# Attention and routed experts on one core: the first batch's expert is guessed from summed values, and work is moved in the written order

## The chip, the core and the metric

The kernel runs on one core of one Trainium2 chip. The metric is the device time of one execution in microseconds (us). TensorE (PE) multiplies matrices, VectorE (DVE), ScalarE (ACT) and GpSimd (POOL) work on tiles, and SyncE (SP) issues most transfers. TensorE's clock has two levels, 1.2 and 2.4 GHz; the profile gives the granted clock as a share of the higher one.

## What is computed

```python
k_p = k.reshape(B, H, Sp, pool, D).mean(axis=3)      # 8 batches, 8 heads, 576 rows, 64 wide, pool 8
v_p = v.reshape(B, H, Sp, pool, D).mean(axis=3)
attn = softmax(scale * q @ k_p.T) @ v_p
x = attn.transpose(0, 2, 1, 3).reshape(B * S, H * D)  # 4608 tokens of 512
g_idx = argmax(x @ w_group); g_w = softmax(...)[g_idx]            # one of 4 groups
e_idx = argmax(x @ w_expert[g_idx]); e_w = softmax(...)[e_idx]    # one of 4 experts in it
out = g_w * e_w * (relu(x @ w1[g, e]) @ w2[g, e])                 # 512 -> 1024 -> 512
```

## The kernel before

The eight batches are worked off one after another. For each batch the attention is computed in five chunks of rows (four of 128 and one of 64), its tokens are routed, and all 576 tokens are run through one expert, the batch's main expert. Tokens of other experts are collected and done in a loop at the end (class Left). The weights and the tokens are each split into a rounded high part and a low part, and three products (high by high, low by high, high by low) replace one exact product.

While batch b runs through its expert, the attention of batch b+1 is computed in the gaps. This order is written out by hand: the strings START, FIRST (batch 0), SECOND (batch 1), STEADY and LAST list pieces of work, `run` (L859) calls them in that order, and each engine gets its instructions in the order in which the pieces issue them (ScalarE from batch 1 on is ordered by the scheduler). In a piece's name the letter says whose it is: `a` attention of the current batch, `m` its expert, `n` the next batch, `w` the next batch's expert, `x` the batch after that, `t` shared. Engines run their queues in order, so a piece that waits holds back all that is behind it on the same engine.

The pieces that matter here:

- `load_k`, `load_v`, `load_q`, `load_qb` (L175 to L219) load keys, values and queries; SP issues them, and ACT a few at the start.
- `kr` (L221) sums eight keys to one by three additions, of two of five column groups (`kr:0`) or three (`kr:1`), on VectorE unless told otherwise; `kt` (L260) turns the sums. `vr` (L240) and `vm` (L245) do the same for values on GpSimd. For batch 0 `vsum` (L250) sums the values on TensorE instead, by eight products with the identity.
- `qt` or `qb` turn queries; `sc`, `mx`, `sb`, `su_`, `nm`, `pt` are the scores, their largest, the exponentials, the sums, the division and the turning of one chunk; `av` and `avd` (L341, L359) multiply by the values and write the tokens' high and low parts.
- `rt`, `route` (L363, L372) give each token its expert by some twenty short VectorE instructions; `count` (L407) counts tokens by expert on TensorE.
- The main expert must be known before its weights can be loaded. For batches 0 and 1 it is guessed from the mean of the values: `guess_x` (L431) multiplies the summed values by small matrices, `guess_r` (L439, batch 0) does so with the unsummed values, `guess_e` (L451) takes the best expert, and SP reads it into a register (L427). Later batches use `main_expert` (L414) after routing.
- `m.load`, `m.cast`, `m.lo`, `m.split` (L503 to L526) load a quarter of a weight matrix, make its high part on ScalarE and its low part on GpSimd. `up` (L528) makes 128 of the 1024 hidden columns for half the tokens with twelve matmuls into one of three PSUM buffers, `upd` (L543) writes the low part of the result on VectorE and so frees the buffer, `down` (L554) is the second layer.
- `warm` (L849) runs matmuls of ones into a PSUM tile that nothing reads.

Of the kernel before, what the change touches and what calls it, by code (L numbers as in the profile page):

```python
# [8 lines left out]
F32 = mybir.dt.float32  # L9
# [25 lines left out]
t.load_wr a.load_k:p a.load_q:0 a.load_v:2 a.load_q:1 a.load_q:4  # L35
t.warm:7 t.turn_wr t.warm:1 a.kr:0 a.qt:0 a.kr:1 a.kt a.sc:0 a.qt:1 a.mx:0 a.sb:0 a.sc:1:m a.mx:1 a.guess_r a.sb:1 a.su_:0 a.nm:0:p a.qt:2 a.guess_e
m.load:1:0 m.load:1:1 m.load:1:2 m.load:1:3 a.vsum n.load_v n.load_k a.su_:1 a.nm:1:p a.pt:0 a.pt:1 a.sc:2:m m.cast:1:0 m.lo:1:0:p:2 a.mx:2 a.sb:2 a.av:0:256
m.cast:1:1 m.lo:1:1:p:2 a.avd:0:256 t.split_wr
# [16 lines left out]
n.pt:3 m.down:4 n.su_:4 n.nm:4:p m.down:5 m.store:1 n.pt:4 x.kr:0 n.av:256:320 n.avd:256:320 x.kr:1 m.down:6 n.rt:256:320 m.down:7 n.route m.down:8 m.store:2 m.down:9 n.main_expert w.load:1:0 w.load:1:1 w.load:1:2 w.load:1:3 m.down:10
x.qb:0 n.gates n.keep_x x.vr:0 x.kt m.down:11 m.store:3 w.split:1:0:p:2 w.load:2:0 x.sc:0 x.mx:0 x.sb:0 x.qb:1 m.down:12 w.split:1:1:p:2 w.load:2:1 x.su_:0 x.nm:0:p m.down:13 m.store:4 x.vr:1 x.vm
# [25 lines left out]
def attn_moe(ctx: ExitStack, tc: tile.TileContext, q, k, v, wg, we, w1, w2, out):  # L82
# [81 lines left out]
    def bc(x, z):  # L164
        return x.unsqueeze(len(x.shape)).broadcast_to(list(x.shape) + [z])

    class Att:
# [203 lines left out]

        def route(s):  # L372

            b = s.b
# [8 lines left out]
            def top1(l, pre):  # L383
                x = sm.tile([128, NC], F32, name="m")
                red(out=x, in_=l, axis=AX.X, op=ALU.max)
                d = sm.tile([128, NC, 4], F32, name="d" + pre)
                tt(out=d, in0=l, in1=bc(x, 4), op=ALU.subtract)
                r = sm.tile([128, NC, 4], F32, name="r" + pre)
                stt(out=r, in0=d, scalar=0.0, in1=desc4.unsqueeze(1).broadcast_to([128, NC, 4]), op0=ALU.is_ge, op1=ALU.mult)
                x = sm.tile([128, NC], F32, name="m2")  # L390
                red(out=x, in_=r, axis=AX.X, op=ALU.max)
                oh = sm.tile([128, NC, 4], F32, name="o" + pre)
                tt(out=oh, in0=r, in1=bc(x, 4), op=ALU.is_equal)
                return oh, d
# [101 lines left out]
    class Moe:  # L496
# [31 lines left out]
        def up(s, f, hf):  # L528
# [303 lines left out]
    class Top:  # L832
# [72 lines left out]
```

## Time and profile before

| | us |
|---|---|
| median of three runs | 587.7 |
| lowest and highest of them | 579.74, 588.12 |
| the profiled execution | 582.81 |
| its span, first to last instruction | 581.1 |

Busy shares of the span: PE 92%, DVE 61%, POOL 42%, ACT 36%. In a table by stage a row has the stretch in us from the span's start, its length, then for PE, PEld (weight loads of TensorE), DVE, ACT and POOL the busy time with the number of instructions, the granted clock, the mean busy share of the transfer engines and GB/s. In a timeline row stand the start, the duration (of all instructions merged into the row), the engine, the line, the operation, the tile written and those read, the shape, the count and, in brackets, how long the engine had been idle and what ended that. L12 is line 12 of the kernel.

### The profile page before, as it was taken

To read this page: it belongs to the slowest core of one execution; us is meant where nothing else is said; L and a number is where in the kernel's file an instruction comes from. 1 tells how busy PE (TensorE), PEld (TensorE's weight loads), DVE (VectorE), ACT (ScalarE), POOL (GpSimd) and SP (SyncE) were. 2 spreads that over 40 slices of the span, in tenths; PEclk is the share of its full clock that TensorE was granted. 3 is DMA by queue.
4 is the path that set the end of the run, shared out by engine and by line. 5 is a ranking of instruction groups with operands and counts; after the bars stand their busy time and mean duration, and the time that the engine had idled before them with its cause. 6 is when DMAs were issued, how large, how long until landed. Compare 5 with 4: busy or idle time off the path is not lost.

```text
span 581.1 us, 15029 instructions
## 1 busy us (share of the span) xinstructions
PE 535.4 (92%) x6081; PEld 462.4 (80%) x6081; DVE 353.7 (61%) x1029; ACT 210.5 (36%) x405; POOL 245.0 (42%) x208
## 2 busy tenths in 40 slices
PE   8988869985999999899989998999999998999995
PEld 3867757765987789789978897889878997899864
DVE  4366567876777587646854595729565672458602
ACT  1234413342322364335532544145423543244111
POOL 2048513256233198136640766075704772231300
PEclk9689979995999999999999999999999999999999
DMA  9179507681706549464843668095746310562831
GB/s 234 33 211 255 89 27 207 178 188 41 179 5 118 175 128 243 75 170 150 229 73 128 186 195 130 30 382 172 162 77 220 101 36 1 181 192 102 276 113 50
DMA packets 114720, 83.44 MB, mean 144 GB/s; under 512 B 69674, under 2 KB 90154, under 8 KB 114264
## 3 DMA queue, kind: packets, MB, share of 16 engines
q1 hardware_dynamic: 110144, 74.37, 48.1%
q10 hardware_dynamic: 4472, 8.04, 4.0%
q8 instruction: 49, 0.80, 0.6%
q14 instruction: 23, 0.19, 0.1%
q0 software_dynamic: 32, 0.04, 0.0%
HBM read 77.14 MB, written 28.38 MB: 182 GB/s over the span
## 4 chain that ended last, share of the span: by engine, by line
PE 75%; DVE 13%; DMA 3%; ACT 3%; issue 2%; POOL 2%; SPq 1%; DVEq 0%; ACTq 0%; POOLq 0%
PE mm L539 29%; PE mm L565 23%; PE sc L300 4%; PE sc L352 4%; PE mm L576 4%; PE tp L369 2%; DMA q<-in_q_dram 2%; POOL w L522 1%; PE tp L444 1%; PE tp L254 1%; DMA sw<-in_moe_w_dram 1%; PE tp L279 1%; DVE xt L361 1%; POOL p L331 1%; PE tp L352 1%
## 5 line engine op out<-in xcount | busy, mean ns | idle before, releaser
L539 PE MATMUL mm<-xt,w 128*128 128x256 f32 (+1 forms) x1536 | 210.6, 295 | 10.0 <-DVE y L582 3.2
L522 POOL TENSOR_TENSOR w<-sw,w 128x1024 fp32r<-128x1024 f32 (+1 forms) x79 | 148.7, 1899 | 163.6 <-ACT w L516 163.6
L539 PEld LDWEIGHTS mm<-xt,w 128*128 128x128 f32 x1536 | 198.7, 194 | 18.2 <-DVE y L582 3.6
L565 PE MATMUL mm<-w,ht 128*128 128x512 f32 x768 | 177.3, 383 | 0.0
L565 PEld LDWEIGHTS mm<-w,ht 128*128 128x128 f32 x768 | 141.5, 189 | 21.6 <-issue 1.9
L541 ACT ACTIVATE ht<-mm 128x256 fp32r<-128x256 f32 (+1 forms) x128 | 52.0, 409 | 96.7 <-PE mm L539 96.5
L331 POOL TENSOR_TENSOR p<-p,su 128x576 f32<-128x576 f32 (+1 forms) x37 | 39.7, 1072 | 104.4 <-DVE su L326 100.8
L516 ACT CAST w<-sw 128x1024 fp32r<-128x1024 f32 x64 | 66.1, 1043 | 23.6 <-DMA sw<-in_moe_w_dram 18.2
L551 DVE SCALAR_TENSOR_TENSOR ht<-mm,ht 128x160 fp32r<-128x160 f32 (+2 forms) x192 | 38.8, 257 | 34.5 <-ACT ht L541 34.0
L311 DVE TENSOR_REDUCE mx<-sc 128x8 f32<-128x576 f32 (+1 forms) x38 | 26.1, 688 | 38.7 <-PE sc L300 38.7
L318 ACT ACTIVATE p<-p 128x576 f32<-128x576 f32 (+1 forms) x40 | 25.5, 637 | 53.4 <-DVE p L316 51.3
L570 ACT ACTIVATE y<-mm,gm 128x512 f32<-128x512 f32 x32 | 21.9, 685 | 58.8 <-PE mm L565 57.4
L352 PE MATMUL sc<-pT,v 32*64 32x256 f32 (+1 forms) x384 | 26.9, 409 | 10.1 <-DVE xt L361 8.1
L547 DVE SCALAR_TENSOR_TENSOR ht<-mm,ht 128x256 fp32r<-128x256 f32 x64 | 26.0, 407 | 15.6 <-ACT ht L541 15.2
L300 PE MATMUL sc<-kT,qT 64*32 64x72 f32 x2176 | 30.6, 229 | 4.0 <-DVE qT L286 2.9
L300 PEld LDWEIGHTS sc<-kT,qT 64*32 64x32 f32 x2176 | 23.9, 105 | 11.7 <-issue 7.4
L338 DVE STREAM_TRANSPOSE pT<-p 128x640 f32<-128x640 f32 (+1 forms) x40 | 30.4, 760 | 3.9 <-POOL p L331 3.9
L324 DVE TENSOR_REDUCE su<-p 128x8 f32<-128x576 f32 (+1 forms) x40 | 27.1, 677 | 5.9 <-ACT p L318 5.7
L576 PE MATMUL mm<-w,ht 128*128 128x512 f32 x128 | 29.6, 381 | 0.0
L352 PE MATMUL tp<-pT,v 32*64 32x256 f32 (+1 forms) x384 | 28.4, 409 | 0.0
L316 DVE TENSOR_TENSOR p<-sc,mx 128x576 f32<-128x576 f32 (+1 forms) x38 | 26.4, 694 | 1.4
L576 PEld LDWEIGHTS mm<-w,ht 128*128 128x128 f32 x128 | 23.9, 189 | 3.8 <-issue 0.5
(203 smaller groups left out, 490.4 us busy)
## 6 DMA issues: line engine op xcount, KB each, us to landing
sw<-in_moe_w_dram SPq DMA_DIRECT2D x72, 512.0 KB
xscr<-xt SPq DMA_DIRECT2D x8, 2304.0 KB
vv<-in_v_dram SPq DMA_DIRECT2D x29, 320.0 KB
q<-in_q_dram SPq DMA_DIRECT2D x112, 72.0 KB
kv<-in_k_dram SPq DMA_DIRECT2D x14, 512.0 KB
out_dram<-y ACTq DMA_DIRECT2D x24, 256.0 KB
pT<-xscr SPq DMA_DIRECT2D x4, 1152.0 KB
out_dram<-y SPq DMA_DIRECT2D x8, 256.0 KB
```

Source lines behind the costliest of these rows:

```text
L300: nc.tensor.matmul(ps[x][32 * g:32 * g + 32, SP * t:SP * t + SP], lhsT=s.qT[c][64 * x:64 * x + 64, g, 32 * t:32 * t + 32], rhs=s.kT[64 * x ...
L324: red(out=su, in_=p.rearrange("p t (x s) -> p t x s", x=2), axis=AX.X, op=ALU.add)
L331: (nc.vector if eng == "v" else nc.gpsimd).tensor_tensor(out=p, in0=p, in1=bc(s.su[c][:, 0:w], SP), op=ALU.mult)
L338: nc.vector.transpose(out=s.pT[:, :, o:o + n].rearrange("p j (t i) -> p t j i", i=32), in_=probs[(s.b * NC + c) % 2][:, 0:n // 32].rearran ...
L352: nc.tensor.matmul(banks[a][64 * x:64 * x + 64, 0:n], lhsT=s.v6[32 * a:32 * a + 32, 5 if x and i == 0 else j, :], rhs=s.pT[32 * a:32 * a + ...
L516: nc.scalar.copy(out=s.w[m, j][0], in_=raw)
L522: (nc.vector if eng == "v" else nc.gpsimd).tensor_tensor(out=wl[:, i:i + n], in0=s.raw[m, j][:, i:i + n], in1=wh[:, i:i + n].bitcast(F32), ...
L539: nc.tensor.matmul(ps[:, 0:n], lhsT=l[:, kc, fs], rhs=apart(xt[:, r, kc, sl]), start=(kc == 0 and i == 0), stop=(kc == 3 and i == 2))
L541: nc.scalar.activation(out=halves(ht[:, sl]), in_=joined(ps[:, 0:n]), func=AF.Relu)
L551: stt(out=ht[:, at:at + hi - lo], in0=ps[:, a, lo:hi], scalar=0.0, in1=ht[:, t + lo:t + hi].bitcast(F32), op0=ALU.max, op1=ALU.subtract)
L565: nc.tensor.matmul(ps, lhsT=s.ht[f][:, 640 * l + o:640 * l + o + 128], rhs=apart(s.w[2, f // 2][r][:, f % 2, :]), start=(i == 0), stop=(i ...
L576: nc.tensor.matmul(ps, lhsT=s.ht[f][:, 512:640], rhs=apart(s.w[2, f // 2][r][:, f % 2, :]), start=(i == 0), stop=(i == 15))
```

## The change

- START: batch 0's values are loaded ahead of its queries and summed on VectorE by a new form of `vr` (all five column groups, three additions), `vm` follows on GpSimd, and the guess uses `guess_x` on the sums. `guess_r` and `vsum` are removed. The guess comes ahead of the second chunk's scores' softmax. `warm` matmuls are half as wide (256 columns), and there are more of them.
- FIRST: batch 1's key sums (`n.kr`) move ahead, from behind the routing to beside `avd` and `upd`; `route` is cut into `route_g` (group) and `route_e` (expert), with expert work between; `count`, `guess_x` and `guess_e` move back by some pieces. Batch 2's key and value sums (`x.kr`, `x.vr`, `x.vm`) move from behind `avd` and from SECOND to ahead of `n.av:256:320`. The division of two chunks moves from GpSimd to VectorE (`:p` to `:v`).
- SECOND: `route_e` and `count` of batch 1 come between its first `up` pieces; `x.vr`, `x.vm` move ahead, `x.kr:1` moves behind `n.route`; two divisions move to VectorE.
- `up` goes through the whole depth for high by high, then high by low part of the tokens, and the weights' low part last.

```diff
@@ -32,28 +32,28 @@
 START = """
-t.load_wr a.load_k:p a.load_q:0 a.load_v:2 a.load_q:1 a.load_q:4
-t.warm:7 t.turn_wr t.warm:1 a.kr:0 a.qt:0 a.kr:1 a.kt a.sc:0 a.qt:1 a.mx:0 a.sb:0 a.sc:1:m a.mx:1 a.guess_r a.sb:1 a.su_:0 a.nm:0:p a.qt:2 a.guess_e
-m.load:1:0 m.load:1:1 m.load:1:2 m.load:1:3 a.vsum n.load_v n.load_k a.su_:1 a.nm:1:p a.pt:0 a.pt:1 a.sc:2:m m.cast:1:0 m.lo:1:0:p:2 a.mx:2 a.sb:2 a.av:0:256
-m.cast:1:1 m.lo:1:1:p:2 a.avd:0:256 t.split_wr
+t.load_wr a.load_k:p a.load_v:2 a.load_q:0 a.load_q:1 a.load_q:4
+t.warm:16 t.turn_wr t.warm:3 a.kr:0 a.kr:1 a.vr:2:f a.kt t.warm:4 a.qt:0 a.qt:1 t.warm:1 a.guess_x a.vm a.sc:0 a.mx:0 a.sb:0 a.guess_e a.sc:1:m
+m.load:1:0 m.load:1:1 m.load:1:2 m.load:1:3 a.mx:1 a.sb:1 a.su_:0 a.nm:0:p a.qt:2 t.warm:4 n.load_v n.load_k a.su_:1 a.nm:1:p a.pt:0 t.warm:6 a.pt:1 m.cast:1:0 m.lo:1:0:p:2 a.sc:2:m
+a.av:0:256 a.mx:2 a.sb:2 m.cast:1:1 m.lo:1:1:p:2 a.avd:0:256 t.split_wr
 FIRST = """
-m.up:5:0 a.pt:4 n.vr:0 m.cast:2:0 m.lo:2:0:p:2 m.upd:5:0 m.up:6:0 m.upd:6:0 m.up:7:0 a.av:256:320 m.upd:7:0 a.rt:0:256 a.avd:256:320
-n.vr:1 n.vm m.up:0:1 m.upd:0:1 a.rt:256:320 m.cast:2:1 m.lo:2:1:p:2 m.up:1:1 m.upd:1:1 m.up:2:1 a.route m.upd:2:1 m.up:3:1 m.cast:2:2 m.lo:2:2:p:2 m.upd:3:1 n.kr:0 n.kr:1 m.up:4:1 a.count m.upd:4:1
-n.guess_x n.kt m.up:5:1 m.upd:5:1 n.guess_e m.cast:2:3 m.lo:2:3:p:2 w.load:1:0 w.load:1:1 n.qb:0 m.up:6:1 m.upd:6:1 n.sc:0 n.mx:0 n.sb:0 n.qb:1 a.gates a.keep_x m.up:7:1 m.upd:7:1
-m.down:0 n.su_:0 n.nm:0:p w.load:1:2 m.down:1 w.load:1:3 m.down:2 n.sc:1 n.mx:1 n.sb:1 n.pt:0 n.qb:2 m.store:0 x.load_v x.load_k m.down:3 w.split:1:0:p:2 n.su_:1 n.nm:1:p m.down:4 n.sc:2 n.mx:2 n.sb:2 n.pt:1 n.qb:3
-m.down:5 m.store:1 w.split:1:1:p:2 n.su_:2 n.nm:2:p n.av:0:256 n.avd:0:256 m.down:6 n.sc:3 n.mx:3 n.sb:3 n.pt:2 n.qb:4 m.down:7 n.su_:3 n.nm:3:v n.rt:0:256 m.down:8 m.store:2
-n.sc:4 n.mx:4 n.sb:4 n.pt:3 w.load:2:0 w.load:2:1 x.load_qb:0 m.down:9 n.su_:4 n.nm:4:v m.down:10 n.pt:4 m.down:11 m.store:3 x.load_qb:1 x.load_qb:2 x.load_qb:3 n.av:256:320 n.avd:256:320 x.kr:0 m.down:12 n.rt:256:320 x.kr:1 m.down:13 m.store:4 n.route
+m.up:5:0 a.pt:4 n.vr:0 m.cast:2:0 m.lo:2:0:p:2 m.upd:5:0 m.up:6:0 m.upd:6:0 m.up:7:0 a.av:256:320 m.upd:7:0 n.kr:0 a.rt:0:256 a.avd:256:320
+n.vr:1 n.vm m.up:0:1 m.upd:0:1 n.kr:1 a.rt:256:320 m.cast:2:1 m.lo:2:1:p:2 m.up:1:1 m.upd:1:1 m.up:2:1 a.route_g m.upd:2:1 m.up:3:1 m.cast:2:2 m.lo:2:2:p:2 a.route_e m.upd:3:1 m.up:4:1 m.upd:4:1
+n.kt m.up:5:1 m.upd:5:1 a.count n.guess_x m.cast:2:3 m.lo:2:3:p:2 n.qb:0 m.up:6:1 n.guess_e w.load:1:0 w.load:1:1 m.upd:6:1 n.sc:0 n.mx:0 n.sb:0 n.qb:1 a.gates a.keep_x m.up:7:1 m.upd:7:1
+m.down:0 n.su_:0 n.nm:0:p w.load:1:2 m.down:1 w.load:1:3 n.sc:1 n.mx:1 n.sb:1 n.pt:0 n.qb:2 m.down:2 m.store:0 x.load_v x.load_k m.down:3 w.split:1:0:p:2 n.su_:1 n.nm:1:v m.down:4 n.sc:2 n.mx:2 n.sb:2 n.pt:1 n.qb:3
+m.down:5 m.store:1 w.split:1:1:p:2 n.su_:2 n.nm:2:v n.av:0:256 n.avd:0:256 m.down:6 n.sc:3 n.mx:3 n.sb:3 n.pt:2 n.qb:4 m.down:7 n.su_:3 n.nm:3:v n.rt:0:256 m.down:8 m.store:2 x.vr:0
+n.sc:4 n.mx:4 n.sb:4 n.pt:3 w.load:2:0 w.load:2:1 x.load_qb:0 m.down:9 n.su_:4 n.nm:4:v m.down:10 n.pt:4 x.kr:0 x.kr:1 x.vr:1 x.vm m.down:11 m.store:3 x.load_qb:1 x.load_qb:2 x.load_qb:3 n.av:256:320 n.avd:256:320 m.down:12 n.rt:256:320 m.down:13 m.store:4 n.route_g
 SECOND = """
-m.up:0:0 m.upd:0:0 m.split:1:2:p:2 m.load:2:2 m.up:1:0 m.upd:1:0 m.split:1:3:p:2 m.load:2:3 m.up:0:1 a.count m.upd:0:1 n.vr:0 m.split:2:0:p:2 m.up:1:1 m.upd:1:1 a.gates a.keep_x m.up:2:0 m.upd:2:0 n.vr:1 n.vm m.up:2:1
+m.up:0:0 m.upd:0:0 m.split:1:2:p:2 m.load:2:2 a.route_e m.up:1:0 m.upd:1:0 m.split:1:3:p:2 m.load:2:3 m.up:0:1 m.upd:0:1 m.split:2:0:p:2 m.up:1:1 a.count m.upd:1:1 a.gates a.keep_x m.up:2:0 m.upd:2:0 m.up:2:1
-n.su_:2 n.nm:2:p m.split:2:3:p:2 m.up:7:1 m.upd:7:1 m.down:0 n.av:0:256 n.avd:0:256 m.down:1 n.sc:3 n.mx:3 n.sb:3 n.pt:2 n.qb:4 m.down:2 m.store:0 n.su_:3 n.nm:3:p x.load_qb:0 x.load_qb:1 x.load_qb:2 x.load_qb:3 m.down:3 n.rt:0:256 n.sc:4 n.mx:4 n.sb:4
-n.pt:3 m.down:4 n.su_:4 n.nm:4:p m.down:5 m.store:1 n.pt:4 x.kr:0 n.av:256:320 n.avd:256:320 x.kr:1 m.down:6 n.rt:256:320 m.down:7 n.route m.down:8 m.store:2 m.down:9 n.main_expert w.load:1:0 w.load:1:1 w.load:1:2 w.load:1:3 m.down:10
-x.qb:0 n.gates n.keep_x x.vr:0 x.kt m.down:11 m.store:3 w.split:1:0:p:2 w.load:2:0 x.sc:0 x.mx:0 x.sb:0 x.qb:1 m.down:12 w.split:1:1:p:2 w.load:2:1 x.su_:0 x.nm:0:p m.down:13 m.store:4 x.vr:1 x.vm
+n.su_:2 n.nm:2:p m.split:2:3:p:2 m.up:7:1 m.upd:7:1 m.down:0 n.av:0:256 n.avd:0:256 m.down:1 n.sc:3 n.mx:3 n.sb:3 n.pt:2 n.qb:4 m.down:2 m.store:0 n.su_:3 n.nm:3:v x.load_qb:0 x.load_qb:1 x.load_qb:2 x.load_qb:3 m.down:3 n.rt:0:256 n.sc:4 n.mx:4 n.sb:4
+n.pt:3 m.down:4 n.su_:4 n.nm:4:v m.down:5 m.store:1 n.pt:4 x.kr:0 n.av:256:320 n.avd:256:320 x.vr:0 m.down:6 n.rt:256:320 m.down:7 n.route x.kr:1 m.down:8 m.store:2 x.vr:1 x.vm m.down:9 n.main_expert w.load:1:0 w.load:1:1 w.load:1:2 w.load:1:3 m.down:10
+x.qb:0 n.gates n.keep_x x.kt m.down:11 m.store:3 w.split:1:0:p:2 w.load:2:0 x.sc:0 x.mx:0 x.sb:0 x.qb:1 m.down:12 w.split:1:1:p:2 w.load:2:1 x.su_:0 x.nm:0:p m.down:13 m.store:4
@@ -237,25 +237,16 @@
                 s.v6 = wk.tile([128, 6, D], F32, name="v6", bufs=2)
             return s.v6
-        def vr(s, u):
-            z = slice(0, 2) if u == 0 else slice(2, 5)
-            a = s.fold(s.v[:, z], nc.gpsimd)
-            nc.gpsimd.tensor_tensor(out=s.vtile()[:, z], in0=a[:, :, 0:64], in1=a[:, :, 64:128], op=ALU.add)
+        def vr(s, u, eng="p"):
+            e = nc.vector if eng == "f" else nc.gpsimd
+            z = (slice(0, 2), slice(2, 5), slice(0, 5))[u]
+            a = s.fold(s.v[:, z], e)
+            e.tensor_tensor(out=s.vtile()[:, z], in0=a[:, :, 0:64], in1=a[:, :, 64:128], op=ALU.add)
         def vm(s):
             for z, at in ((1, 5), (0, 2)):
                 nc.gpsimd.tensor_tensor(out=s.v6[:, at, :], in0=s.v6[:, 2, :], in1=share[:, z:z + 1].broadcast_to([128, D]), op=ALU.mult)
-
-        def vsum(s):
-
-            ps = ps_t.tile([128, 512], F32, name="tp")
-            for j in range(8):
-                nc.tensor.matmul(ps[:, 0:NC * D], lhsT=ident, rhs=s.v[:, :, D * j:D * j + D], start=(j == 0), stop=(j == 7))
-            v6 = s.vtile()
-            nc.scalar.copy(out=v6[:, 0:NC], in_=ps[:, 0:NC * D].rearrange("p (j d) -> p j d", d=D))
-            for z, at in ((1, 5), (0, 2)):
-                nc.scalar.activation(out=v6[:, at, :], in_=ps[:, 2 * D:3 * D], func=AF.Copy, scale=share[:, z:z + 1])
         def kt(s):
             ps = [ps_t.tile([128, 512], F32, name="tp") for i in range(2)]
@@ -369,8 +360,24 @@
+        def top1(s, l, pre):
...
         def route(s):
 
+            s.route_g()
+            s.route_e()
+
+        def route_g(s):
@@ -380,29 +387,20 @@
-            def top1(l, pre):
...
-            goh, gd = top1(lg[:, :, 0:4], "g")
+            goh, s.gd = s.top1(lg[:, :, 0:4], "g")
+            s.goh = goh
+
+        def route_e(s):
+            goh, lg = s.goh, lgs[s.b % 2]
+            eoh, ed = s.top1(el, "e")
+            s.d = (s.gd, ed)
...
@@ -435,18 +433,6 @@
-
-        def guess_r(s):
-
-            ps = ps_t.tile([128, 512], F32, name="tp")
-            for t in range(NC):
-                for j in range(4):
-                    nc.tensor.matmul(ps[:, 0:8], lhsT=s.v[:, t, 128 * j:128 * j + 128], rhs=heads[:, :, t, :], start=(t == 0 and j == 0), stop=(t == 4 and j == 3))
-            s.gx = sm.tile([128, NG], F32, name="gx", bufs=1)
-            odd = sm.tile([128, NC, E], F32, name="el").rearrange("p c e -> p (c e)")[0:64, 0:8]
-            nc.scalar.copy(out=odd, in_=ps[64:128, 0:8])
-            for x in range(2):
-                tt(out=s.gx[64 * x:64 * x + 64], in0=ps[0:64, 4 * x:4 * x + 4], in1=odd[:, 4 * x:4 * x + 4], op=ALU.add)
@@ -534,8 +520,8 @@
             o, n = HALF[hf]
             sl = slice(o, o + n)
             ps = s.pu[f, hf] = ps_m.tile([128, 512], F32, name="mm")
-            for kc in range(4):
-                for i, (l, r) in enumerate(((wh, 0), (wl, 0), (wh, 1))):
+            for i, (l, r) in enumerate(((wh, 0), (wh, 1), (wl, 0))):
+                for kc in range(4):
                     nc.tensor.matmul(ps[:, 0:n], lhsT=l[:, kc, fs], rhs=apart(xt[:, r, kc, sl]),
                                      start=(kc == 0 and i == 0), stop=(kc == 3 and i == 2))
             nc.scalar.activation(out=halves(ht[:, sl]), in_=joined(ps[:, 0:n]), func=AF.Relu)
@@ -850,7 +836,7 @@
             ps = ps_m.tile([128, 512], F32, name="mm")
             for i in range(z):
-                nc.tensor.matmul(ps, lhsT=ones, rhs=ones.unsqueeze(1).broadcast_to([128, 4, 128]), start=True, stop=True)
+                nc.tensor.matmul(ps[:, 0:256], lhsT=ones, rhs=ones.unsqueeze(1).broadcast_to([128, 2, 128]), start=True, stop=True)
     left, top = Left(), Top()
     att = [Att(b) for b in range(B)] + [None] * 2
```


## Rows read from the trace of the kernel before

**Rows 1.** Busy time by stage: length, five engines, clock, DMA share, GB/s.
```profile
0.00:40.00 40.00, 35.23 (x379) 24.80 (x379) 17.19 (x49) 9.17 (x20) 7.95 (x23) 0.83 0.57 155
...
70.00:88.00 18.00, 11.75 (x138) 10.20 (x137) 12.65 (x35) 3.35 (x8) 5.00 (x4) 0.81 0.11 35
...
125.00:147.00 22.00, 12.84 (x69) 11.81 (x68) 16.85 (x40) 5.72 (x12) 15.32 (x15) 0.69 0.30 74
147.00:194.00 47.00, 46.38 (x625) 39.62 (x624) 35.62 (x98) 14.74 (x33) 13.01 (x12) 1.00 0.43 99
```

**Rows 2.** Timeline of START: start, duration, engine, line, operation, tiles, [idle before <- releaser].
```profile
12.36 1.09 PE L279 MATMUL tp<-ident,q 128*64 128x128 f32 x16 [0.93 <-DMA q<-in_q_dram]
...
18.13 7.40 PE L444 MATMUL tp<-heads,vv 128*128 128x8 f32 x40
...
25.46 1.98 PE L279 MATMUL tp<-ident,q 128*64 128x128 f32 x16
...
29.10 6.60 PE L254 MATMUL tp<-vv,ident 128*128 128x320 f32 x16
...
30.43 0.15 DVE L426 TENSOR_SCALAR me<-ct 128x1 int32<-128x1 f32 x1
...
31.60 2.13 SPq L510 DMA_DIRECT2D sw<-in_moe_w_dram  x4
...
42.13 0.38 ACT L541 ACTIVATE ht<-mm 128x256 fp32r<-128x256 f32 x1 [1.09 <-PE mm L539]
```

**Rows 3.** Waits of TensorE, 70 to 88 us: total, times, longest.
```profile
PE tp L263 <- DVE kb L227: 2.9, 2, 1.6
...
PE tp L410 <- DVE oh L404: 1.3, 1, 1.3
```

**Rows 4.** Waits of TensorE, 125 to 147 us.
```profile
PE tp L410 <- DVE oh L404: 6.0, 1, 6.0
PE mm L539 <- DVE y L582: 3.2, 1, 3.2
```

**Rows 5.** Busy time by stage, as rows 1: the end of the first transfers.
```profile
15.00:20.00 5.00, 4.32 (x155) 3.86 (x134) 2.34 (x4) 1.27 (x2) 0.00 (x0) 0.96 0.29 65
```

**Rows 6.** Timeline, 57 to 84 us, second half of batch 0's hidden layer.
```profile
59.74 0.82 DVE L361 TENSOR_TENSOR xt<-sc,xt 128x640 fp32r<-128x640 f32 x1 [1.69 <-ACT xt L357]
...
72.10 0.75 PE L435 MATMUL tp<-heads,v 128*64 128x4 f32 x20
72.65 0.70 DVE L231 TENSOR_TENSOR kv<-kv 128x512 f32<-128x512 f32 x1
...
74.19 0.95 DVE L231 TENSOR_TENSOR kv<-kv 128x768 f32<-128x768 f32 x1
...
77.30 3.57 PE L539 MATMUL mm<-xt,w 128*128 128x320 f32 x12
...
81.65 1.88 PE L539 MATMUL mm<-xt,w 128*128 128x320 f32 x12
```

**Rows 7.** Busy time by stage, as rows 1: the end of batch 2's values and keys.
```profile
110.00:112.00 2.00, 2.00 (x12) 1.51 (x9) 1.90 (x5) 0.37 (x1) 0.00 (x0) 1.00 0.00 0
```

**Rows 8.** Timeline, 120 to 148 us, from batch 0's last half to batch 1's hidden layer.
```profile
120.43 0.82 DVE L361 TENSOR_TENSOR xt<-sc,xt 128x640 fp32r<-128x640 f32 x1 [4.33 <-ACT xt L357]
...
122.07 6.49 POOL L522 TENSOR_TENSOR w<-sw,w 128x512 fp32r<-128x512 f32 x4 [15.42 <-ACT w L516]
...
125.40 2.03 DVE L231 TENSOR_TENSOR kv<-kv 128x768 f32<-128x768 f32 x1
...
134.03 1.80 POOL L231 TENSOR_TENSOR vv<-vv 128x768 f32<-128x768 f32 x1
...
134.36 1.52 DVE L393 TENSOR_TENSOR og<-rg,m 128x20 f32<-128x20 f32 x1
...
140.17 7.61 PE L539 MATMUL mm<-xt,w 128*128 128x320 f32 x36
```

**Rows 9.** Timeline of SyncE, 194 us: batch 2's expert weights.
```profile
194.68 2.31 SPq L510 DMA_DIRECT2D sw<-in_moe_w_dram  x4
```

More of the change, by code (lines that the diff above doesn't have):

```diff
@@ L370, in rt @@
             nc.scalar.copy(out=halves(s.lt[0:40, sl]), in_=joined(ps[0:40, 0:n]))
+        def top1(s, l, pre):
+            x = sm.tile([128, NC], F32, name="m")
+            red(out=x, in_=l, axis=AX.X, op=ALU.max)
+            d = sm.tile([128, NC, 4], F32, name="d" + pre)
+            tt(out=d, in0=l, in1=bc(x, 4), op=ALU.subtract)
+            r = sm.tile([128, NC, 4], F32, name="r" + pre)
+            stt(out=r, in0=d, scalar=0.0, in1=desc4.unsqueeze(1).broadcast_to([128, NC, 4]), op0=ALU.is_ge, op1=ALU.mult)
+            x = sm.tile([128, NC], F32, name="m2")
+            red(out=x, in_=r, axis=AX.X, op=ALU.max)
+            oh = sm.tile([128, NC, 4], F32, name="o" + pre)
+            tt(out=oh, in0=r, in1=bc(x, 4), op=ALU.is_equal)
+            return oh, d
         def route(s):
+            s.route_g()
+            s.route_e()
+        def route_g(s):
             b = s.b
@@ L381, in route @@
             red(out=lg[0:64, 4, :], in_=lpv[0:64, 4], axis=AX.X, op=ALU.add)
-            def top1(l, pre):
[L384 to L394, printed above, removed]
-            goh, gd = top1(lg[:, :, 0:4], "g")
+            goh, s.gd = s.top1(lg[:, :, 0:4], "g")
             tt(out=goh, in0=goh, in1=bc(valid, 4), op=ALU.mult)
+            s.goh = goh
+        def route_e(s):
+            goh, lg = s.goh, lgs[s.b % 2]
             es = sm.tile([128, NC, G, E], F32, name="es", bufs=1)
@@ L401, in route @@
             red(out=el, in_=es.rearrange("p c g e -> p c e g"), axis=AX.X, op=ALU.add)
-            eoh, ed = top1(el, "e")
+            eoh, ed = s.top1(el, "e")
             s.oh = sm.tile([128, NC, G, E], F32, name="oh")
             tt(out=s.oh, in0=bc(goh, E), in1=eoh.unsqueeze(2).broadcast_to([128, NC, G, E]), op=ALU.mult)
-            s.d = (gd, ed)
+            s.d = (s.gd, ed)
         def count(s):
```

## The prediction

> **What bounds the kernel now.** I read the busy time by stage first. From 147 us on TensorE is busy for 46.4 of 47 us at the higher clock level, and nothing in the diff takes a matmul away there, so that part can hardly move. Three earlier stages are different [rows 1]. In START TensorE counts as busy for 35 of 40 us, but the granted clock averages 0.83 and the first product of batch 0's expert has its result taken out only at 42.13 [rows 2]. From 70 to 88 TensorE is busy for 11.75 of 18 us, from 125 to 147 for 12.84 of 22, both partly at the lower level [rows 1].
>
> Next, the timeline of START [rows 2]. The guess from unsummed values holds TensorE for 7.40 us from 18.13, the turning of a query chunk takes 1.98 us, and only at 31.60 does SP issue the expert's weights: it needs the expert's number, written at 30.43. Then the summing of values on TensorE takes another 6.60 us, and the attention product waits for it. In the same view a turning that took 1.09 us at 12.36 takes 1.98 at 25.46: the lower level. So the reader should see one chain in START, from values to guess to weights to first product, with 14.00 us (7.40 + 6.60) of TensorE work that feeds the guess and the sums.
>
> Then TensorE's waits in the other two stages. From 70 to 88 it waits 2.9 us for the summed keys (`kb`) and 1.3 for the routing's last result (`oh`) [rows 3]; afterwards twelve matmuls take 3.57 us where they soon take 1.88 [rows 6]: the idle time is followed by the lower level. From 125 to 147 it waits 6.0 us for `oh` and 3.2 for `y`, both on VectorE [rows 4], which has batch 2's key sums ahead of them in its queue [rows 8]. What these stages lose:
> - 70 to 88: 18.0 - 11.75 = 6.25 idle, and 3.57 - 1.88 = 1.69 at the lower level: 7.9 us.
> - 125 to 147: 22.0 - 12.84 = 9.16 idle, and 36 matmuls took 7.61 where three times 1.88 is 5.64, so 1.97: 11.1 us.
>
> **The change part by part.**
>
> *START: earlier guess.* New on the path are the values' sums on VectorE. A fold of 512 columns takes 0.70 us, one of 768 takes 0.95 [rows 6]; on that line 1280, 640 and 320 columns take about 1.45, 0.83 and 0.5, so 2.8 us. Values now move ahead of queries. The first transfers die out at about 16.5 us (0.29 of the stretch from 15 to 20 [rows 5]), and the bytes are the same, so the last queries needed land by about 16, while the keys and values, two thirds of the bytes, are there by about 12; the sums are done by 15, hidden behind the queries. From 16: turning a chunk 1.09 [rows 2], one warm piece 0.3 (two matmuls at 1.88 / 12), `guess_x` 0.75 [rows 6], so 18.2. Before, from the end of `guess_r` (25.53) to the loads took 31.60 - 25.53 = 6.07, of which 1.98 was a query chunk's turning. In its place come the first scores, which I count like a turning at 12.36, 1.09: 5.2 us. The loads come at 23.4, 8.2 earlier. From the loads to the first result took 42.13 - 31.60 = 10.53 us; `vsum` is gone from it, while the first two chunks' softmax is now partly behind the guess on VectorE. I take 9.8. The first result is then out at 33.2: a gain of 8.9, say 9. Bounds: 5, if queries arrive late and all this runs at the lower level; 10, if the softmax is no limit. The added `warm` matmuls are ahead of the queries' arrival; without that cover each piece would cost its 0.3.
>
> What the weights trigger (the other weight quarters, batch 1's values, keys and queries) is issued by SP in the same order, so it all moves forward with the loads. It costs nothing as long as these transfers keep their distance from their users.
>
> *Batch 0's second half.* The key sums of batch 1 go from between the routing and `kt` to two earlier places, so the 2.9 us wait goes, `count` stands one `up` later, and `upd` pieces come between the halves of the routing. Late next: `avd`. `n.kr:0` takes 1.54 us alone (72.65 to 74.19) and VectorE idles 1.69 us before `avd` [rows 6], so alone it would be free. But GpSimd is then summing batch 1's values, and where the two engines overlapped a 768-column fold took 2.03 instead of 0.95 [rows 6, 8], 2.1 times. So 1.54 x 2.1 = 3.3, and `avd`, with the product behind it, is 3.3 - 1.69 = 1.6 late. The routing will meet GpSimd too: one short instruction took 1.52 us, to the end of GpSimd's 1.80 us one [rows 8], where another short one takes 0.15 [rows 2]; I count one such wait, 1.4. Gain: 7.9 - 1.6 - 1.4 = 4.9, say 5. Bounds: 0, if each short instruction meets GpSimd, and 7.9.
>
> The Trainium skill (SBUF — State Buffer, section Who interferes with whom) says that a VectorE instruction with two SBUF inputs and a GpSimd instruction that reads SBUF exclude each other, the later one waiting out the whole of the other. The row at 134.36 agrees, ending where GpSimd's does [rows 8]. By that rule alone each of `kr`'s three additions could wait for one GpSimd instruction, and `avd` would be later than I count.
>
> *From batch 0's last half to batch 1.* Batch 2's key sums go ahead of `avd`, where VectorE idles 4.33 us; its value sums go ahead on GpSimd, which idles 15.42 us [rows 8]. Both need transfers, which are over by 110 us: the DMA share is 0.00 there [rows 7]. So I cost both moves at nothing; if that cover failed, `avd` and the next batch's first products would queue behind the wait for keys. VectorE then comes to `y` and the routing right after `avd`: the 3.2 us wait for `y` goes whole, that for `oh` mostly [rows 4]. What stays is routing beside GpSimd's low parts: one and a half waits of 1.4, 2.1. Gain: 11.1 - 2.1 = 9.0. Bounds: 4, if most of the two-input instructions wait, and 11.1.
>
> *Batch 2's expert.* In SECOND `x.kr:1` goes behind `n.route` and so ahead of the count on VectorE: 0.95 for its first addition and, by `kr:0`'s other two (1.54 - 0.70 = 0.84 on two column groups, so 1.26 on three), 2.2 in all [rows 6], by which the loads at 194.68 [rows 9] come later, less what VectorE waits for the count anyway. I take 1.0 lost. Bounds: 0 and 2.2.
>
> *The rest.* `up`'s new order has the same matmuls and lets a piece start before the low part is there: nothing, since TensorE is full from 147 on [rows 1]. Divisions on VectorE instead of GpSimd, and `vm` on GpSimd while it idles: nothing, within the idle times above.
>
> **Sum.** 9 + 5 + 9 - 1 = 22. Against the profiled execution's 582.8: 560.8, say 561. That execution lies 4.9 below the median of the runs, 587.7, and inside their spread of 579.74 to 588.12, so the median could come out a few us higher too.
>
> **The rivals.**
> 1. *The stalls mostly stay, through the shared access of VectorE and GpSimd.* For it: 1.52 and 2.03 us rows [rows 8], and both stages keep GpSimd's work. Against it: the wait's main part was queueing behind key sums, which go. Gains 1 and 4 instead of 5 and 9: 582.8 - (9 + 1 + 4 - 1) = 569.8, so 570. The skill's rule above is this rival's. Chance 0.20.
> 2. *The guess is not much earlier*, because queries, pushed behind values, arrive late. For it: TensorE already waited 0.93 us for the first queries at 12.36 [rows 2]. Against: the bytes end at the same time [rows 5]. START gains 5: 565. Chance 0.10.
> 3. *START's gain is partly given back* since the stalls are set by something that does not move, such as transfers: total 8, so 575. Against: the transfers' share is 0.11 and 0.30 in the two stages [rows 1]. Chance 0.08.
> 4. *Not faster: TensorE stays at the lower level* through batch 0's hidden layer, since START now has short work with waits for queries between. Price: 1.69 us for each twelve matmuls [rows 6], 16 such pieces. At 13 of them the 22 us are gone: 583; all 16: 588. For it: the turning at 25.46 ran at that level [rows 2], and START's mean clock was 0.83 [rows 1]. Against: most of the slow work is removed, and the clock was back for the first products. Chance 0.05.
>
> **How the numbers follow.** My forecast has 0.57 (553 to 566 by itself). 582.8 - (10 + 7.9 + 11.1) = 553.8, all upper bounds at once with nothing lost at batch 2, so 553. The range 553 to 573 takes in rivals 1 and 2 and leaves out 3, 4 and a tail below. About 2% can be told from no change: 2% below the median is 576. Forecast and rivals 1 and 2 lie below it, 0.87, and rival 3 only just, by 1, so that I count a part of it on either side: I give faster 0.88, within 2% 0.09, slower 0.03.
>
> **What would show it.** In the profile after: the weights' first issue near 23 us and the first result near 33; no lines of `guess_r` and `vsum`; TensorE's waits for `kb` gone, and for `oh` and `y` after batch 0 below 2 us; the granted clock near 1.00 in those two stages. `avd` some 1.6 us late beside GpSimd's sums, and batch 2's weights issued later against its routing. I would be wrong if the queries land after 18 us, if the clock is low from 23 to 60 us, or if VectorE waits for batch 2's keys ahead of `avd`.

## The result, and the profile after

The changed kernel takes 559.64 us (median of four runs, 557.66 to 561.11) against 585.72 of the kernel before, beside which it ran: a ratio of 0.957, interval 0.948 to 0.965. The forecast was 561. Its profiled execution has a span of 559.4 us, 21.7 less than before's 581.1.

Busy time by stage of the kernel after (columns as rows 1), in stretches that answer to those of rows 1:

```profile
0.00:31.50 31.50, 28.06 (x398) 22.83 (x398) 19.49 (x51) 8.00 (x16) 8.66 (x25) 1.00 0.73 196
...
62.00:75.00 13.00, 12.87 (x168) 11.96 (x167) 9.93 (x41) 4.94 (x10) 6.17 (x5) 1.00 0.01 3
...
112.00:126.00 14.00, 11.24 (x67) 10.78 (x68) 10.69 (x39) 5.43 (x11) 6.69 (x6) 0.79 0.39 107
126.00:171.00 45.00, 44.81 (x615) 38.41 (x614) 32.12 (x85) 14.74 (x33) 15.17 (x15) 0.99 0.43 98
```

START now has a mean granted clock of 1.00, and the stage that was 18 us long with 6.25 idle is 13 us with 0.13 idle. Between batches 0 and 1 a hole remains: 2.76 us idle and a clock of 0.79. From then on TensorE is as full as before.

The timeline of START (columns as rows 2):

```profile
13.43 1.49 DVE L231 TENSOR_TENSOR vv<-vv 128x1280 f32<-128x1280 f32 x1 [2.81 <-DMA vv<-in_v_dram]
...
15.00 1.97 PE L270 MATMUL tp<-ident,q 128*64 128x128 f32 x32 [0.67 <-DMA q<-in_q_dram]
...
17.53 0.75 PE L433 MATMUL tp<-heads,v 128*64 128x4 f32 x20
...
22.96 2.11 SPq L496 DMA_DIRECT2D sw<-in_moe_w_dram  x4
...
33.02 0.38 ACT L527 ACTIVATE ht<-mm 128x256 fp32r<-128x256 f32 x1
```

The value sums are three VectorE instructions from 13.43; the queries' turning starts at 15.00, the guess on the sums at 17.53, the weights are issued at 22.96 instead of 31.60, and the first result is taken out at 33.02 instead of 42.13 [rows 2]. What TensorE still waits for, from 31 to 62 and from 110 to 126 us (columns as rows 3):

```profile
PE mm L525 <- DVE xt L352: 2.1, 1, 2.1
...
PE tp L408 <- DVE oh L402: 2.8, 1, 2.8
```

The wait for `kb` [rows 3] and that for `y` [rows 4] are gone, that for `oh` fell from 6.0 to 2.8, and one for `avd`'s result is new.

Where the time came from, by the same event in both traces (us from the span's start):

| event | before | after | gained so far | in this stretch |
|---|---|---|---|---|
| first result of batch 0's expert taken out | 42.13 | 33.02 | 9.1 | 9.1 |
| batch 0's second attention product | 57.10 | 49.16 | 7.9 | -1.2 |
| its second layer starts | 88.18 | 75.11 | 13.1 | 5.1 |
| `kt` of batch 2 | 147.62 | 126.97 | 20.7 | 7.6 |
| batch 2's expert weights issued | 194.68 | 175.19 | 19.5 | -1.2 |
| end | 581.1 | 559.4 | 21.7 | 2.2 |

These are two single executions: before's lies 2.9 us below its median and after's 1.5 above, so that the medians differ by 26.1 and the events by 21.7.

### The profile page after: what moved, and what is told of

It reads as the page before. It is cut to its first block, busy times and chain, and to the rows that moved or that the text cites. A ratio compares the mean times of both kernels' runs of the same rounds, so it can differ in the third digit from the quotient of the medians.

```text
span 559.4 us, 15062 instructions
## 1 busy us (share of the span) xinstructions
PE 526.1 (94%) x6097; PEld 459.1 (82%) x6097; DVE 358.2 (64%) x1034; ACT 209.4 (37%) x402; POOL 242.0 (43%) x206
## 4 chain that ended last, share of the span: by engine, by line
PE 72%; DVE 16%; DMA 5%; ACT 2%; issue 2%; POOL 1%; SPq 0%; ACTq 0%; POOLq 0%; DVEq 0%
PE mm L525 31%; PE mm L551 22%; PE mm L562 4%; PE sc L291 4%; PE sc L343 4%; PE tp L360 3%; DMA q<-in_q_dram 2%; DVE p L307 1%; DVE pT L329 1%; DMA sw<-in_moe_w_dram 1%; DMA out_dram<-y 1%; DVE mx L302 1%; DVE su L315 1%; DVE xt L352 1%; DVE p L322 1%
## 5 line engine op out<-in xcount | busy, mean ns | idle before, releaser
L551 PEld LDWEIGHTS mm<-w,ht 128*128 128x128 f32 x768 | 141.5, 189 | 21.6 <-issue 1.5
L502 ACT CAST w<-sw 128x1024 fp32r<-128x1024 f32 x64 | 66.1, 1043 | 22.3 <-DMA sw<-in_moe_w_dram 21.4
L322 POOL TENSOR_TENSOR p<-p,su 128x576 f32<-128x576 f32 (+1 forms) x33 | 35.6, 1079 | 80.2 <-DVE su L317 70.4
L343 PEld LDWEIGHTS sc<-pT,v 32*64 32x64 f32 x384 | 14.0, 131 | 16.7 <-issue 11.7
```

The source lines that it names most:

```text
L322: (nc.vector if eng == "v" else nc.gpsimd).tensor_tensor(out=p, in0=p, in1=bc(s.su[c][:, 0:w], SP), op=ALU.mult)
L343: nc.tensor.matmul(banks[a][64 * x:64 * x + 64, 0:n], lhsT=s.v6[32 * a:32 * a + 32, 5 if x and i == 0 else j, :], rhs=s.pT[32 * a:32 * a + ...
L502: nc.scalar.copy(out=s.w[m, j][0], in_=raw)
L551: nc.tensor.matmul(ps, lhsT=s.ht[f][:, 640 * l + o:640 * l + o + 128], rhs=apart(s.w[2, f // 2][r][:, f % 2, :]), start=(i == 0), stop=(i ...
```

## The experiments

The theory under test: three separate holes, each closed for its own reason, so that the gains add up; what is left of them is VectorE waiting for GpSimd. Times are medians of four runs. Gaps are to the 559.64 of the changed kernel, which did not run beside any of the experiments. Two kernels that differ from it little served as its twins: `old_up_order` (560.30) ran beside `start_alone`, `moves_alone` and `keys_behind`, and `xkr_ahead` (558.83) beside `route_late`, `div_on_dve` and `all_three`. `values_behind` and `no_late_warm` had only the kernel before beside them (581.21).

**START alone.** The new START (with the new `vr` and narrower `warm`) in the kernel before.

> The changed START alone, all else as before (only the two forms of vr and the narrower warm matmuls come with it). My theory, three separate gains that add up: about 9 us less than before, some 574, with the first result out near 33 us and the waits at the routing as before. Rival, START's gain is given back because batch 0's hidden layer is set by something that does not move: less than 4 us. Rival, the stalls grow without the moves: the sum of this kernel's gain and that of the moves alone stays well under the whole change's 22 us.

573.67 against 584.03 beside it: ratio 0.979 (0.971 to 0.987), 10.4 us; faster, but the interval leaves open whether by 2%. In its trace the weights are issued at 23.40 and the first result is out at 33.19. The other two holes are as before; TensorE's waits from 32 to 70 and from 100 to 150 us:

```profile
PE tp L264 <- DVE kb L227: 3.1, 2, 1.6
...
PE tp L411 <- DVE oh L405: 6.7, 1, 6.7
PE mm L540 <- DVE y L583: 3.2, 1, 3.2
```

**The moves alone.** The old START with everything else of the change.

> The old START (guess from unsummed values, sums on TensorE, wide warm matmuls) with all moves of the change in the later strings, the routing in two pieces and the new order in up. My theory: about 13 us less than before, some 570 (5 in batch 0's second half, 7 to 9 between batches 0 and 1). Rival: the moves only pay because START changed the distance between transfers and their users: less than 8 us.

568.15 against the same 584.03: ratio 0.971 (0.963 to 0.978), 15.9 us. The two gains add to 26.3; the whole change has 26.1 between its medians. By the intervals each gain is known to about 4.5 us only. Within that they add up, and the rivals by which one part eats most of the other's gain fall.

**The old order in `up`.**

```diff
-            for i, (l, r) in enumerate(((wh, 0), (wh, 1), (wl, 0))):
-                for kc in range(4):
+            for kc in range(4):
+                for i, (l, r) in enumerate(((wh, 0), (wl, 0), (wh, 1))):
```

> The changed kernel with up's old order (high by high, low by high, high by low for each depth step). My theory as forecast: within 1 us of the changed kernel, as the matmuls are the same. Rival: the order is worth 2 us, because at batch 2's first products, where weights arrive late, the low parts are waited for; then the loss shows between the load of batch 2's expert weights and the first scores after it, and nowhere else.

560.30 against 559.64 of the changed kernel: the same. From the issue of batch 2's weights to the end its trace takes 384.9 us, against 384.2 in the changed kernel and 386.4 before, so most of the 2.2 us gained there does not come from this order.

**Key sums behind `avd`.**

```diff
-m.upd:7:0 n.kr:0 a.rt:0:256 a.avd:256:320
+m.upd:7:0 a.rt:0:256 a.avd:256:320 n.kr:0
```

> The changed kernel with batch 1's first key sums put behind avd instead of ahead of it. Theory of the shared access: VectorE's three additions wait for GpSimd's value sums and hold avd back, the wait of TensorE for xt of 2.1 us goes, and the kernel is about 2 us faster. Rival: the wait only moves to the upd pieces behind avd or to kt, and the time is the same within 1 us.

556.39, so 3.3 us faster, more than expected. In the changed kernel's timeline the three additions of the key sums and GpSimd's instructions take turns:

```profile
49.97 1.83 POOL L231 TENSOR_TENSOR vv<-vv 128x768 f32<-128x768 f32 x1
...
50.03 2.32 DVE L231 TENSOR_TENSOR kv<-kv 128x512 f32<-128x512 f32 x1
...
51.88 1.33 POOL L232 TENSOR_TENSOR vv<-vv 128x384 f32<-128x384 f32 x1
...
52.38 1.10 DVE L232 TENSOR_TENSOR kv<-kv 128x256 f32<-128x256 f32 x1
53.28 0.65 POOL L244 TENSOR_TENSOR v<-vv 128x192 f32<-128x192 f32 x1
53.52 0.69 DVE L227 TENSOR_TENSOR kb<-kv 128x256 f32<-128x256 f32 x1
...
54.14 0.81 DVE L352 TENSOR_TENSOR xt<-sc,xt 128x640 fp32r<-128x640 f32 x1
...
55.00 2.50 PE L525 MATMUL mm<-xt,w 128*128 128x320 f32 x8 [2.12 <-DVE xt L352]
```

The additions need 2.32, 1.10 and 0.69 us, 4.2 from the start of the first to the end of the last, and the first two end 0.55 and 0.27 us after the GpSimd instruction that ran beside them; `avd` begins at 54.14 and the product at 55.00. TensorE's wait of 2.1 us is followed by the lower level: the granted clock is 0.54 in the 2 us from 55.00. With the sums behind, `avd` starts 2.6 us after the attention product (49.05) instead of 5.0 (49.16), and the stretch from that product to the second layer takes 22.3 us instead of 26.0:

```profile
51.68 0.82 DVE L352 TENSOR_TENSOR xt<-sc,xt 128x640 fp32r<-128x640 f32 x1 [1.69 <-ACT xt L348]
...
53.22 0.76 DVE L231 TENSOR_TENSOR kv<-kv 128x512 f32<-128x512 f32 x1
```

**The value sums behind instead.** The same hole from the other side: VectorE keeps its order, GpSimd's part beside it goes.

```diff
-n.vr:1 n.vm m.up:0:1 m.upd:0:1 n.kr:1 a.rt:256:320 m.cast:2:1 m.lo:2:1:p:2
+m.up:0:1 m.upd:0:1 n.kr:1 a.rt:256:320 m.cast:2:1 m.lo:2:1:p:2 n.vr:1 n.vm
```

> The changed kernel; batch 1's first key sums stay ahead of avd on VectorE, but GpSimd's value sums that ran beside them (three of five column groups, and the two shares) stand behind the next weight quarter's low part. Theory of the shared access: the key sums take about 1.6 us instead of 4.2, TensorE's wait for xt of 2.1 us goes, and 2 to 4 us are gained, less what the routing loses when it meets the value sums later. Rival, the key sums are simply too long for the gap ahead of avd: they stay long and the wait stays, no gain.

556.23, 3.4 us faster, though one of its four runs took 559.22. The same three additions in the same place:

```profile
49.33 0.68 DVE L231 TENSOR_TENSOR kv<-kv 128x512 f32<-128x512 f32 x1
...
50.05 0.42 DVE L232 TENSOR_TENSOR kv<-kv 128x256 f32<-128x256 f32 x1
...
50.50 0.42 DVE L227 TENSOR_TENSOR kb<-kv 128x256 f32<-128x256 f32 x1
...
51.10 0.82 DVE L352 TENSOR_TENSOR xt<-sc,xt 128x640 fp32r<-128x640 f32 x1 [0.17 <-ACT xt L348]
```

0.68, 0.42 and 0.42: without a neighbour on GpSimd they take 1.5 us and fit ahead of `avd`, which now waits only 0.17 us, for its input from ScalarE. So it was the neighbour and not the length of the key sums. But not all of the 3.4 us comes from here: the stretch from the attention product to the second layer took 24.3 us, 1.6 less than in the changed kernel, where `keys_behind` took 3.7 less. The loss that I expected came: the count behind the routing, for which TensorE does not wait there in the changed kernel, now waits 1.79. More of the shorter profiled time lies between batches 0 and 1, where nothing was moved. There the count waits as before, but the lower level did not follow (in the changed kernel the same 24 matmuls took 5.96, as the next experiment shows):

```profile
118.38 0.45 PE L408 MATMUL tp<-oh,ones 128*128 128x80 f32 x2 [2.76 <-DVE oh L402]
118.71 3.24 PE L525 MATMUL mm<-xt,w 128*128 128x256 f32 x24
```

The three additions show the cause; what moving the value sums is worth by itself is known less well. The exclusion of the two engines is the one that the Trainium skill describes (SBUF — State Buffer, Who interferes with whom), and as that rule had it, `avd` was later than I counted: 2.4 us, not 1.6.

**Routing and count later.** Between batches 0 and 1.

```diff
-... m.down:13 m.store:4 n.route_g
+... m.down:13 m.store:4
-m.load:2:2 a.route_e m.up:1:0 ... m.upd:0:1 m.split:2:0:p:2 m.up:1:1 a.count m.upd:1:1 a.gates a.keep_x m.up:2:0 m.upd:2:0 m.up:2:1
-m.upd:2:1
+m.load:2:2 m.up:1:0 ... m.upd:0:1 a.route_g m.split:2:0:p:2 m.up:1:1 m.upd:1:1 a.route_e m.up:2:0 m.upd:2:0 m.up:2:1
+a.count m.upd:2:1 a.gates a.keep_x
```

> The changed kernel; in SECOND both routing pieces of batch 1 come behind three up and upd pieces, and the count, gates and keep_x behind up:2:1. Theory: what is left between batches 0 and 1 (2.8 us wait for oh, then the lower level: 24 matmuls in 5.96 us) comes from the count standing in TensorE's queue ahead of work that is ready; the wait and the low level both go, 4 to 5 us faster. Rival: up pieces are held by their PSUM buffers, which VectorE frees only behind the routing's waits for GpSimd; then the wait only changes its name, and the gain is under 2.

556.21, 3.4 us faster, between theory and rival (2.6 under its twin `xkr_ahead`). First the hole in the changed kernel:

```profile
108.77 9.92 POOL L508 TENSOR_TENSOR w<-sw,w 128x512 fp32r<-128x512 f32 x8 [7.02 <-ACT w L502]
...
115.07 1.20 DVE L369 SCALAR_TENSOR_TENSOR rg<-dg,desc 128x20 f32<-128x20 f32 x1
...
116.52 0.98 DVE L373 TENSOR_TENSOR og<-rg,m 128x20 f32<-128x20 f32 x1
...
117.53 1.19 DVE L391 TENSOR_TENSOR og<-og,valid 128x20 f32<-128x20 f32 x1
...
120.72 0.71 PE L408 MATMUL tp<-oh,ones 128*128 128x80 f32 x2 [2.76 <-DVE oh L402]
...
121.17 5.96 PE L525 MATMUL mm<-xt,w 128*128 128x256 f32 x24
```

GpSimd makes eight half low parts without a break; three short VectorE instructions of the routing take 1.20, 0.98 and 1.19 us; the count waits 2.76; and 24 matmuls after it take 5.96 us. With the later count TensorE's wait is

```profile
PE tp L408 <- DVE oh L402: 1.2, 1, 1.2
```

so 1.2 are left, and the low level is gone: the granted clock is 1.00 in the 8 us from 121. That the low level follows a wait of this length is not certain, though. Eight traces have the same wait of about 2.76 us for the count; the low level follows in six (24 matmuls in 4.50 to 5.96 us, where they stand together) and not in `values_behind` and `no_late_warm` (3.24). The changed kernel's profiled execution has the longest, and in its four runs the mean clock goes from 0.989 to 0.997 while the time falls from 561.11 to 557.66. So the wait is a property of the order, and what the clock adds to it differs from one execution to the next.

**One division on VectorE.** `a.nm:2:p` becomes `a.nm:2:v`.

> The changed kernel with one division (batch 0's third chunk) on VectorE instead of GpSimd. The changed kernel gains 9.1 us up to the first result but only 7.9 up to batch 0's second attention product. Theory: 1.2 us are given back because that division stands on GpSimd behind the low part of the second weight quarter, and VectorE waits 1.96 us to turn the chunk; here the time from the first up to that product falls from 18.7 to about 17.5, total 1 us less. Rival: the transfers of the next batch set this stretch; no change.

559.26 against 559.64: nothing, and from the first `up` to the second attention product 18.4 instead of 18.7 us. The theory was half right: the wait it names is there, but little of the time came back. The chain that ended last shows the stretch; the changed kernel (start, duration, what):

```profile
34.07 1.29 POOL w L508
35.36 1.12 POOL p L322
36.48 0.02 issue
36.50 0.84 DVE pT L329
```

The chunk's division indeed stands behind a low part. With the division on VectorE the same chain reads

```profile
33.91 1.00 DVE wrs L833
34.91 1.76 DVE p L322
36.67 0.34 DVE ht L533
37.00 0.75 DVE pT L329
```

A short VectorE instruction (`wrs`) and the division meet the same low parts there, at 1.00 and 1.76 us. The wait moved, it did not go. From here to the second attention product neither chain has a transfer in it; both go through the chunks' softmax.

**Batch 3's key sums ahead of batch 2's routing again.**

```diff
-x.vr:0 m.down:6 n.rt:256:320 m.down:7 n.route x.kr:1 m.down:8
+x.kr:1 x.vr:0 m.down:6 n.rt:256:320 m.down:7 n.route m.down:8
```

> The changed kernel with batch 3's second key sums put back ahead of batch 2's routing, as in the kernel before, so that VectorE reaches the count earlier. As forecast: the expert weights of batch 2 are issued 1.2 us sooner against kt of the batch before, and the time falls by 1. Rival: the lateness is hidden, since weights issued sooner only wait for transfers or for the last products; the issue is sooner and the time is the same within 0.7.

SyncE's issue in the changed kernel and here:

```profile
175.19 2.30 SPq L496 DMA_DIRECT2D sw<-in_moe_w_dram  x4
```

```profile
172.55 2.30 SPq L496 DMA_DIRECT2D sw<-in_moe_w_dram  x4
```

Against `kt` of batch 2 (126.97 and 125.67) that is 48.2 and 46.9 us: 1.3 sooner. The time is 558.83, 0.8 less, with runs of 557.19 to 559.98 against 557.66 to 561.11. Theory (1 us) and rival (within 0.7) lie too close together to be told apart by these runs. The traces don't settle it either: from `kt` to the end it takes 431.7 us against 432.4, and 432.8 and 433.1 in `div_on_dve` and `old_up_order`, which have the late order too. Whether the lateness is hidden stays open.

**Without the later `warm` pieces.** The four pieces `t.warm:4`, `t.warm:1`, `t.warm:4` and `t.warm:6` behind `kt` are dropped (30 matmuls in the trace); they feed nothing.

> The changed kernel without the warm matmuls that stand behind kt in START (five pieces of 4, 1, 4 and 6; those of the beginning stay). They feed nothing. Theory: TensorE then idles between the short products, the clock falls to the lower level, and START's short products and the first up pieces run at it: the weights are issued up to 1 us later and the whole is 1 to 4 us slower. Rival: the clock is held by the other work; the first weights come as early or earlier, since no warm piece stands ahead of the guess, and the time is the same.

563.67, 4.0 us slower than 559.64 (559.76 to 564.91), though the weights are issued at 21.49 instead of 22.96. Busy time by stage, 25 to 36 us, here and then in the changed kernel:

```profile
25.00:31.00 6.00, 3.75 (x48) 1.66 (x48) 2.72 (x6) 1.04 (x1) 3.51 (x3) 0.53 1.02 284
31.00:36.00 5.00, 4.55 (x35) 4.10 (x28) 3.77 (x9) 3.25 (x8) 1.96 (x2) 0.54 1.07 202
```

```profile
25.00:31.00 6.00, 4.38 (x122) 3.02 (x120) 4.42 (x10) 2.03 (x5) 4.59 (x4) 1.00 1.03 333
31.00:36.00 5.00, 5.00 (x89) 4.21 (x93) 3.47 (x9) 4.17 (x8) 3.20 (x3) 1.00 1.08 191
```

The granted clock is 0.53 and 0.54 against 1.00, and the first `up` starts at 31.68 instead of 30.44. My fourth rival, the lower level in START, was a real mechanism; the `warm` pieces keep it away.

But the trace does not put the 4.0 us there. The second layer starts at 76.20 instead of 75.11, 1.1 later. `kt` of batch 2 comes at 125.20 instead of 126.97, earlier, as the lower level did not follow the count's wait in this execution. The loss lies behind the issue of batch 2's weights: 388.8 us from there to the end against 384.2, with a wait for a weight quarter and a low clock behind it that the changed kernel's trace has not:

```profile
180.59 1.16 PE L525 MATMUL mm<-xt,w 128*128 128x256 f32 x8 [1.71 <-ACT w L502]
```

```profile
185.00:190.00 5.00, 5.00 (x34) 4.91 (x24) 4.02 (x9) 2.00 (x5) 4.01 (x3) 0.58 0.75 227
```

Whether that comes from the missing pieces was not tried. What is shown is the level in START and about 1.1 us for it in one execution; the rest of the 4.0 is not explained.

**All three.** Key sums behind, routing and count later, the division on VectorE.

> Key sums behind avd, both routing pieces and the count later, and the third chunk's division on VectorE, all at once on the changed kernel. If the three sit in different stretches they add up: 3.3 + 4 + 1, some 551. If GpSimd and VectorE only trade places, no better than 555.

552.95 (552.31 to 553.49), ratio to the kernel before 0.952 (0.948 to 0.955), 6.7 us under the changed kernel and 5.9 under its twin `xkr_ahead`, which ran beside it. Within the runs' spread the two gains of 3.3 and 3.4 add up, the division adds nothing that can be told. It beats both kernels. The 24 matmuls behind the count take 3.24 us here instead of 5.96:

```profile
118.03 0.45 PE L408 MATMUL tp<-oh,ones 128*128 128x80 f32 x2 [1.19 <-DVE oh L402]
...
119.05 3.24 PE L525 MATMUL mm<-xt,w 128*128 128x256 f32 x24
```

## Why the prediction was right, step by step

- **START, 9.** The weights were forecast for 23.4 and came at 22.96, the first result for 33.2 and came at 33.02: 9.1. Inside, errors cancel: the queries were there at 15.00 and not at 16, but two chunks are turned ahead of the guess (1.97 us) where I counted one (1.09), and the value sums ended at 16.30 and not by 15, hidden all the same. But 1.2 of the gain is given back before the second attention product, which I had not seen. The chain there goes through the softmax of the later chunks, and in the new START the third chunk's exponentials (31.07 on ScalarE) stand behind the casts of the first attention product (30.01), where they stood ahead of them before (38.18 and 38.77). That this order is the cause is read from the rows and was not tried by itself. The step "what the weights trigger moves forward with the loads" was right for transfers and incomplete for VectorE. Worth: 7.9.
- **Batch 0's second half, 5.** Measured 5.1, by two errors that cancel, so the number is in part luck. The term "`avd` 1.6 late" was mis-sized: `avd` was 2.4 late, as the key sums stretched 2.7 times (4.2 for 1.54) and not 2.1, and with the lower level behind TensorE's wait the sums in that place cost 3.3 us. The 1.4 for the routing was not lost: its waits (0.99 and 1.26 at the end of `route_e`) lay beside full TensorE work.
- **Between batches 0 and 1, 9.** Measured 7.6. The cover for batch 2's sums held: its key additions took 0.65 and 0.95, without a neighbour, and nothing waited for them. The term "one and a half waits, 2.1" was too small: there were three, of 0.8 to 1.0 us each (1.20, 0.98 and 1.19 where such an instruction takes 0.18 elsewhere in the trace), and I left out the lower level that can follow them, worth 5.96 - 3.24 = 2.7 on the next 24 matmuls in this execution, although rows 6 and 8 show just this. Two of the signs that I named failed here: the wait for `oh` is 2.8 and not below 2, and the stage's clock is 0.79. With less of the lower level the same stretch gained 8.8 to 9.0 in `old_up_order`, `xkr_ahead` and `div_on_dve`, near the forecast.
- **Batch 2's expert, -1.** The weights are issued 1.2 us later, as forecast; whether that costs anything stays open (`xkr_ahead`). From the issue to the end the changed kernel is even 2.2 shorter. Which of the other moves in SECOND this comes from was not tried and stays open; executions differ there (386.4 us from issue to end in the kernel before, 385.0 in START alone, which has the same SECOND).
- **`up`'s order, 0.** Right.
- **The sum.** 7.9 + 5.1 + 7.6 + 1.0 = 21.7 by the events' exact times, for a forecast 22. The medians differ by more, 26.1; the forecast time of 561 rests on before's profiled execution, which lies below its median, as I had said. The rivals: the shared access is real and, with the low level that can follow its waits, cost up to some 6 us of what was to be had, as `all_three` shows, but not enough to bring rival 1's 570; late queries (rival 2) showed as a wait of 0.7 us for the first chunk; rival 3 falls with the two halves adding up; rival 4 did not come, for the reason above.

## What to carry to other kernels

When work is moved into an idle gap of VectorE, look at what GpSimd does in that gap: two-input additions of 1.5 us cost 4.2 beside GpSimd's. Price a move by the stretch after it too: a gain at one event can be partly given back when another engine's chain sets the next event. A wait of TensorE costs more than its length where the clock falls after it, which one trace can show and the next not: look at several before putting a price on it. Matmuls that feed nothing can hold the clock (1.00 against 0.53 in START); what that is worth has to be read from the events behind it, and not from the total alone.

## What the hardware showed that I had not expected

VectorE and GpSimd took turns instruction by instruction, and a VectorE addition of 0.68 us took 2.32 when it was issued just after a 1.83 us GpSimd one. Leaving out 30 matmuls without a use put the clock at 0.53 from 25 to 36 us: the weights were issued 1.5 us earlier, and the first product came 1.2 later. The same wait of TensorE, about 2.76 us, was followed by the lower level in six traces and not in two.
